# K projections in 64-row TensorE tiles, with the order of a fused linear-attention and gated-FFN kernel drawn anew

## The chip, the cores and the metric

The kernel runs on one core of a Trainium2 chip. The metric is the device time of one execution in microseconds (us), as the median of several executions. Before the change it is 396.28 us (three runs, 396.02 to 397.35). The profiled execution has a span of 394.4 us from its first to its last instruction.

## The reference, cut to what matters

The program is an attention layer without a softmax over the sequence, followed by a gated feed-forward network (FFN). There are 8 batches, 8 heads, 576 rows a head, head dimension 64 and 128 features.

```python
def phi(x):                                  # q and k alike
    proj = np.einsum('bhsd,df->bhsf', x, w_phi)          # 64 -> 128
    proj = proj - np.max(np.abs(proj), axis=-1, keepdims=True)
    return np.concatenate([np.exp(proj), np.exp(-proj)], axis=-1)
q_p, k_p = phi(q), phi(k)
kv  = einsum('bhsf,bhsd->bhfd', k_p, v);  z = sum(k_p, axis=2)
out = (q_p @ kv) / (q_p @ z + 1e-06)
...
gate = np.maximum(x @ w_gate, 0.0);  val = x @ w_val     # 512 -> 1536, on 4608 rows
return gate * val @ w_out                                # 1536 -> 512
```

The contraction of the projection (`x @ w_phi`) is only 64 deep, while TensorE has 128 rows. That mismatch is what the change is about.

## The kernel before

The work is cut into small pieces: K projections, scaled V, K-by-V products, Q projections, numerators, half-steps of the FFN. A class `Plan` holds for each piece a list of engines with rough durations and the buffers that it takes and frees. The order in which the pieces are issued is a literal list of numbers, `ORDER`, which was annealed offline on that model and is replayed when the kernel is built. All PSUM tiles come from one pool of eight banks.

A K item is four transposed blocks of K. A block has 128 partitions: the 64 dimensions of one chunk of rows in partitions 0 to 63 and those of another chunk in 64 to 127. `w2` is a block-diagonal matrix: `w_phi` in the upper left half, `w_phi` in the lower right half, zeros elsewhere. So one full 128-row matmul of 256 columns projects both chunks, and half of what it multiplies is zero. A K item is issued in two pieces of two matmuls and one bank each:

```python
def project_rows(T2, m):                     # K, before: 128-row matmuls with zeros
    pp = psum_a()
    for i in range(2):
        nc.tensor.matmul(pp[:, 2*F*i : 2*F*(i+1)],
                         lhsT=T2[:, i, :], rhs=w2.rearrange("p a f -> p (a f)"))   # L287
    nc.vector.tensor_reduce(m, pp..., op=ALU.max, apply_absolute_value=True)       # L292
    return pp

def k_rows(st, i):                           # called for i = 0 and i = 1
    pp = project_rows(st["T"][:, 2*i : 2*i+2], st["m"][:, 4*i : 4*i+4])
    kp = st["pool"].tile([P, 2, 4, F], BF16, name=f"kp{i}")
    for s, sign in ((0, 1.0), (1, -1.0)):
        nc.scalar.activation(kp[:, s]..., pp, AF.Exp, scale=sign)                  # L322
    ...
    if i == 1:                               # the row factors, once for the item
        ek = ...; two small nc.scalar.activation(ek[:, :, s], st["m"], AF.Exp)     # L329
```

Q already uses 64-row tiles. A Q group first projects by columns (two matmuls of 512 columns, one for each half of the rows), then by rows (eight matmuls of 128 columns, alternating between the upper and the lower 64 rows, each half into its own bank):

```python
def q_group(st, i, places, first):
    ...
    for par in range(2):
        rows = slice(D*par, D*(par+1))
        nc.tensor.matmul(cols[par]..., lhsT=w2[rows, par, :], rhs=T4[rows])        # L382
    banks = [psum_a(), psum_a()]
    for j in range(4):
        for par in range(2):
            rows = slice(D*par, D*(par+1))
            nc.tensor.matmul(banks[par][:, F*j : F*(j+1)],
                             lhsT=T4[rows, j, :], rhs=w2[rows, par, :])            # L389
    ...                                      # 4 exps on ScalarE (L397), 2 row maxima on VectorE
```

The other TensorE lines are the K-by-V products (L363, 20 matmuls an item), the numerators (L420), the first FFN products with the value and the gate weights (L487), the second FFN product (L506), transposes (L267, L459) and filler matmuls on zeros that keep the clock up while nothing else can run in the first 45 us (L840).

In the model, a piece on TensorE had only its own duration:

```python
for i, op in enumerate(ops):
    eng, us = op[:2]
    src = op[2] if len(op) > 2 else i - 1
    t = max(free[eng], ready if src is None or not i else ends[src])
    ...
# K: [("PE", 0.23), ("DVE", 0.6), ("ACT", 0.48, 0), ("ACT", 0.48, 0)], one bank, twice an item
# Q: [("PE", 0.66)] + ..., four banks
```

Of the kernel before, what the change touches and what calls it, by code (L numbers as in the profile page):

```python
# [19 lines left out]
class Plan:  # L20
# [10 lines left out]
    def __init__(self, slots):  # L31
        self.slots = {tag: [0.0] * n for tag, n in slots.items()}
        self.free = dict.fromkeys(self.LAG, 0.0)
        self.done = {}
        self.uses = {}
        self.pieces = []
# [6 lines left out]
    def times(self, piece):  # L43
# [12 lines left out]
        for i, op in enumerate(ops):  # L56
            eng, us = op[:2]
            src = op[2] if len(op) > 2 else i - 1
            t = max(free[eng], ready if src is None or not i else ends[src])
            if len(op) > 4:  # L60
                t = max(t, self.done[op[4]])
            if eng == "NONE":
                t = ready if src is None or not i else ends[src]
            if start is None:
                start = t
            free[eng] = t + us
            ends.append(t + us + (op[3] if len(op) > 3 else self.LAG[eng]))
        return start, ready, ends, free

    def emit(self, piece, got):  # L70
        _, _, fn, ops, _, gives, take, drop, _, at = piece
        _, _, ends, self.free = got
        for tag in take:
            self.slots[tag].pop(0)
# [14 lines left out]
    def order(self):  # L89
# [3 lines left out]
        for i in map(int, ORDER.split()):  # L93
            piece = self.pieces[i]
            got = self.times(piece)
            assert got is not None
            now, start = self.free["PE"], got[0]
            if piece[3][0][0] == "PE" and start < self.BUSY_TILL and self.slots["pa"][0] <= now:
                n = int((start - now - 0.25) / (0.43 if now < 8.0 else 0.22))
                if n > 0:  # L100
                    self.slots["pa"].append(self.slots["pa"].pop(0))
                    got = self.times(piece)
                    yield lambda n=n: self.keep_busy(n)
            yield self.emit(piece, got)


ORDER = """40 41 42 0 1 4 45 55 46 50 56 43 57 58 47 51 2 60 61 7 48 62 52 63 65 76 53 66 3 59 64 10 49 87 92
67 54 102 44 93 5 88 94 72 6 8 73 74 95 89 68 69 97 70 77 78 96 71 75 107 90 83 14 79 439 80 13 91
440 9 81 84 85 441 442 443 444 445 446 447 448 103 143 449 82 11 141 86 450 12 98 99 451 118 452
149 453 454 455 100 456 457 458 104 459 17 460 108 461 159 101 462 463 105 129 464 465 109 466 106  # L110
467 136 468 110 111 112 469 470 471 114 472 115 473 474 116 119 475 154 120 476 477 137 478 121 150
125 479 15 480 18 16 138 113 126 130 481 122 123 127 155 142 186 164 482 483 131 484 485 124 23 144
486 117 128 156 151 160 188 139 132 21 487 488 489 145 490 491 492 152 493 157 161 494 146 495 147
133 19 496 497 153 165 162 158 498 134 193 499 166 20 198 140 22 148 500 163 189 194 501 171 199
167 502 503 195 168 200 504 169 505 506 507 230 175 508 244 187 509 190 510 170 172 196 173 174 203
176 191 231 511 201 219 512 242 177 204 205 197 513 182 178 206 208 514 515 183 179 516 245 180 184
181 202 185 28 192 232 207 517 24 237 238 239 518 27 250 233 25 519 209 246 520 521 234 522 210 523
235 255 260 524 26 525 32 211 526 212 527 215 528 135 529 247 287 213 251 530 531 532 236 248 533
256 534 535 304 261 536 241 537 240 538 262 214 539 540 220 216 541 542 543 221 263 544 545 243 217
276 546 252 249 289 226 218 253 227 264 547 33 228 229 257 222 265 258 548 549 223 224 305 550 551  # L120
299 225 552 266 254 553 554 306 555 294 267 259 300 556 557 29 307 558 31 295 301 559 268 272 560
345 288 561 562 343 346 563 269 270 564 565 566 302 567 296 273 34 568 277 271 569 570 571 309 572
297 278 573 290 274 574 575 283 35 576 279 284 577 578 285 308 579 580 356 581 280 582 275 281 310
298 291 583 584 286 585 311 586 351 303 292 282 587 588 347 293 357 589 590 30 316 338 591 312 592
339 344 593 340 313 361 594 320 348 36 314 595 596 597 331 598 599 600 321 38 388 601 341 602 603
604 605 358 366 606 359 607 317 322 608 332 318 609 610 352 323 611 612 353 613 324 614 615 333 390
315 354 616 617 327 618 325 362 328 319 360 326 329 619 620 363 330 621 355 334 39 622 349 623 624
367 391 625 626 350 627 432 628 389 364 368 335 405 365 629 630 336 395 369 410 631 370 371 632 433
633 406 377 634 37 635 407 636 637 373 342 638 639 396 640 641 642 643 374 378 644 400 645 372 397
398 337 646 647 379 648 649 392 375 650 384 399 401 393 651 385 652 653 654 386 394 380 421 402 381  # L130
655 656 657 382 387 411 376 658 408 383 659 660 412 661 662 409 663 403 664 404 665 666 413 417 667
668 669 414 415 670 671 672 673 674 422 675 676 677 423 678 418 679 680 681 682 428 683 424 429 684
430 685 686 419 687 688 416 420 689 690 434 431 425 426 691 692 693 435 427 694 695 696 697 698 699
700 701 702 436 703 704 705 706 707 708 709 710 711 712 713 714 715 716 717 718 719 720 721 722 723
724 725 726 437 438 727 728 729 730 731 732 733 734 735 736 737 738 739 740 741 742 743 744 745 746
747 748 749 750 751 752 753 754 755 756 757 758 759 760 761 762 763 764 765 766 767 768 769 770 771
772 773 774"""
# [6 lines left out]
def kernel(  # L144
# [138 lines left out]
    def project_rows(T2, m):  # L283

        pp = psum_a()
        for i in range(2):
            nc.tensor.matmul(  # L287
                pp[:, 2 * F * i : 2 * F * (i + 1)],
                lhsT=T2[:, i, :],
                rhs=w2.rearrange("p a f -> p (a f)"),  # L290
            )
        nc.vector.tensor_reduce(  # L292
            m,
            pp.rearrange("p (c f) -> p c f", f=F),
            axis=AX.X,
            op=ALU.max,
            apply_absolute_value=True,
        )
        return pp

# [11 lines left out]
    def k_start(st, T, pool):  # L312
        st["T"] = T
        st["pool"] = pool
        st["kp"] = []
        st["m"] = sb_s.tile([P, 8], FP32, name="mk")

    def k_rows(st, i):
        pp = project_rows(st["T"][:, 2 * i : 2 * i + 2], st["m"][:, 4 * i : 4 * i + 4])
        kp = st["pool"].tile([P, 2, 4, F], BF16, name=f"kp{i}")  # L320
        for s, sign in ((0, 1.0), (1, -1.0)):
            nc.scalar.activation(  # L322
                kp[:, s].rearrange("p c f -> p (c f)"), pp, AF.Exp, scale=sign
            )
        st["kp"].append(kp)
        if i == 1:
            ek = st["ek"] = sb_s.tile([P, 8, 2], FP32, name="ek")
            for s, sign in ((0, -1.0), (1, 1.0)):
                nc.scalar.activation(ek[:, :, s], st["m"], AF.Exp, scale=sign)  # L329
# [19 lines left out]
    def k_kv(st, b, u, copy):  # L349
# [4 lines left out]
        for hh in range(2):  # L354
            h = 2 * u + hh
            for s in range(2):
                for c in range(C + 1):
                    if c < C:
                        lhsT, rhs = st["kp"][hh][:, s, c, :], st["vs"][:, 4 * hh + c, s, :]
                    else:  # L360
                        lhsT = mixed["kp"][h // 4][:, s, h % 4, :]
# [13 lines left out]
    def q_group(st, i, places, first):  # L375
# [9 lines left out]
        banks = [psum_a(), psum_a()]  # L385
        for j in range(4):
            for par in range(2):
                rows = slice(D * par, D * (par + 1))
                nc.tensor.matmul(  # L389
                    banks[par][:, F * j : F * (j + 1)], lhsT=T4[rows, j, :], rhs=w2[rows, par, :]  # L390
                )
# [189 lines left out]
    def k_pieces(rank, st, start, ops, needs, take, name, late=()):  # L581
        plan.add(rank, "kT", start, ops, needs, (rank, "T"), take, late)
        for i in range(2):
            ops = [("PE", 0.23), ("DVE", 0.6), ("ACT", 0.48, 0), ("ACT", 0.48, 0)]
            if i == 1:
                ops.append(("ACT", 0.4, 1))
            plan.add(
                rank,
                "krows",
                lambda i=i: k_rows(st, i),  # L590
                ops,
                [(rank, "T")],
                (rank, "rows", i),
                ["pa"],
                [("pa", 3)] + [(tag, 0, n, key) for tag, n, key in name],
                [(rank, "rows", 0)] if i else [],
            )

    def k_item(rank, b, u):
# [14 lines left out]
        if by_dma:  # L614
            k_pieces(
                rank, st, start, [("NONE", 0.0)], [("knT", b)], ["kp"], [(f"knT{b % 2}", 2 * NU, b)]
            )
        else:
# [7 lines left out]
                [("T4", 2, rank)],  # L626
# [7 lines left out]
            [(rank, "rows", 1), (rank, "rows", 0), ("vn", b, u == 0) if b == 0 else ("vn", b)],  # L634
# [15 lines left out]
    def k_item_mixed(rank, i):  # L650
# [11 lines left out]
        if by_dma:  # L662
            k_pieces(rank, st, start, [("NONE", 0.0)], [("kmT", i)], ["km"], [("kmT", 2, i)])
        else:
# [7 lines left out]
                [("T4", 2, rank)],  # L672
                [("pa", 1), ("kmn", 0)],
            )
        for bb in range(2):
# [6 lines left out]
                [(rank, "rows", 1), (rank, "rows", 0), ("vm", i)],  # L682
# [4 lines left out]
    def q_pieces(rank, turned, ops, needs, take, late, name, cols, chunks, first, by_dma):  # L687
# [7 lines left out]
        for i, places in enumerate(cols):  # L695
# [7 lines left out]
                [("PE", 0.66)]  # L703
# [266 lines left out]
```

## Time and profile before

| what | value |
|---|---|
| time, median of 3 | 396.28 us |
| span of the profiled execution | 394.4 us, 8456 instructions |
| TensorE clock granted, mean | 0.998 |
| VectorE busy | 254.1 us |
| ScalarE busy | 245.3 us |
| GpSimd busy | 156.3 us |
| DMA | 45.04 MB, 114 GB/s on average |

The page lists busy times of each engine (PE is TensorE, PEld its weight loads, DVE VectorE, ACT ScalarE, POOL GpSimd), the span in 40 slices, the chain of work that ended last, and groups of instructions by source line, with what ended the idle time before them. A matmul's duration in such a list includes its way through the array, which overlaps with its successor; what a block of matmuls costs TensorE is therefore read from the start of the block to the start of the next one, which the timeline gives.

### The profile page before, as it was taken

How to read it: one execution, taken by the hardware profiler on the slowest of the kernel's cores; microseconds unless marked ns; L12 is line 12 of the kernel's file. 1: busy time of each engine (PE TensorE's matmuls, PEld its weight loads, DVE VectorE, ACT ScalarE, POOL GpSimd, SP SyncE). 2: the span in 40 equal slices, each digit the busy share in tenths (PEclk: the TensorE clock that was granted, in tenths of full speed). 3: DMA queues.
4: the chain of work that ended last, by engine and by line, in shares of the span. 5: the costliest groups of instructions: out<-in, count | busy, mean ns of one | idle time of the engine just before them, and what ended most of it. 6: DMA issues, size and time to landing. Idle time of an engine off the chain costs nothing.

```text
span 394.4 us, 8456 instructions
## 1 busy us (share of the span) xinstructions
PE 378.1 (96%) x3220; PEld 207.1 (53%) x3269; DVE 254.1 (64%) x570; ACT 245.3 (62%) x563; POOL 156.3 (40%) x202
## 2 busy tenths in 40 slices
PE   6978999999999999999999999999999999999994
PEld 3566855556556545544555455555554444444442
DVE  2789767868988969667746776777736744422420
ACT  2887584688988677777486766578647333323321
POOL 2899652268574365625252437225511210010000
PEclk9999999999999999999999999999999999999999
DMA  7989999999958992599559705630220031011003
GB/s 227 196 147 193 178 154 132 182 167 215 121 102 157 302 162 55 109 172 228 82 93 193 89 15 95 173 82 2 56 95 13 6 89 55 0 53 69 0 22 84
DMA packets 91801, 45.04 MB, mean 114 GB/s; under 512 B 57842, under 2 KB 87154, under 8 KB 91762
## 3 DMA queue, kind: packets, MB, share of 16 engines
q1 hardware_dynamic: 62994, 30.88, 36.7%
q0 software_dynamic: 28768, 13.63, 29.3%
q8 instruction: 25, 0.41, 0.4%
q14 instruction: 14, 0.11, 0.1%
HBM read 37.81 MB, written 9.44 MB: 120 GB/s over the span
## 4 chain that ended last, share of the span: by engine, by line
PE 88%; POOL 5%; DVE 2%; issue 2%; ACT 1%; DMA 1%; SPq 0%; ACTq 0%; DVEq 0%
PE pf L487 46%; PE pf L506 24%; PE pa L420 5%; PE pa L363 4%; PE pa L287 3%; PE pa L382 3%; PE pa L389 2%; POOL vs L304 2%; DMA wf<-in_w_phi_dram 1%; ACT kp L322 1%; POOL vsm L304 1%; DVE mk L292 1%; DVE h L498 1%; POOL wv_sb L251 1%; PE pa L267 1%
## 5 line engine op out<-in xcount | busy, mean ns | idle before, releaser
L498 DVE SCALAR_TENSOR_TENSOR h<-pf,val_sb 128x512 bf16<-128x512 f32 (+1 forms) x114 | 74.5, 658 | 67.4 <-PE pf L487 46.7
L496 ACT CAST val_sb<-pf 128x512 bf16<-128x512 f32 (+1 forms) x114 | 63.9, 576 | 62.7 <-PE pf L487 59.3
L322 ACT ACTIVATE kp<-pa 128x512 bf16<-128x512 f32 x144 | 77.5, 607 | 39.1 <-DVE mk L292 38.9
L506 PE MATMUL pf<-wo_sb,h 128*128 128x512 bf16 x412 | 98.8, 379 | 1.0
L487 PE MATMUL pf<-xT,wg_sb 128*128 128x512 bf16 (+1 forms) x397 | 98.9, 366 | 0.7
L487 PE MATMUL pf<-xT,wv_sb 128*128 128x512 bf16 (+1 forms) x392 | 98.3, 366 | 0.7
L449 POOL TENSOR_TENSOR xu<-u,r 128x512 bf16<-128x512 f32 x36 | 37.4, 1042 | 146.0 <-DVE r L447 65.3
L304 POOL TENSOR_TENSOR vs<-vn,ek 128x512 bf16<-128x512 f32 x64 | 65.8, 1050 | 27.7 <-ACT ek L329 27.7
L397 ACT ACTIVATE qp<-pa 128x512 bf16<-128x512 f32 x128 | 66.4, 623 | 4.5 <-PE pa L382 4.5
L487 PEld LDWEIGHTS <-wv_sb 128*128 128x128 bf16 x456 | 42.5, 98 | 42.2 <-DMA out_dram<-out_sb 0.2
L487 PEld LDWEIGHTS <-wg_sb 128*128 128x128 bf16 x456 | 42.2, 98 | 40.1 <-issue 0.3
L506 PEld LDWEIGHTS <-h 128*128 128x128 bf16 x432 | 40.0, 98 | 41.4
L292 DVE TENSOR_REDUCE mk<-pa 128x4 f32<-128x512 f32 x72 | 47.7, 679 | 10.5 <-PE pa L287 10.2
L275 DVE TENSOR_REDUCE mq<-pa 128x4 f32<-128x512 f32 x72 | 45.7, 680 | 11.6 <-PE pa L389 11.4
L436 DVE TENSOR_TENSOR t<-pa,cq 128x195 f32<-128x195 f32 (+3 forms) x120 | 39.5, 329 | 17.7 <-PE pa L420 17.0
L444 DVE TENSOR_TENSOR u<-pa,t 128x195 f32<-128x195 f32 (+3 forms) x120 | 40.5, 338 | 6.8 <-DVE t L436 0.5
L516 ACT COPY out_sb<-pf 128x512 f32<-128x512 f32 x36 | 21.4, 594 | 32.5 <-PE pf L506 30.3
L420 PEld LDWEIGHTS <-qp 128*128 128x128 bf16 x640 | 30.7, 98 | 14.5 <-issue 0.4
L420 PE MATMUL pa<-kv,qp 128*128 128x65 bf16 x640 | 33.9, 193 | 0.2
L363 PEld LDWEIGHTS <-kp 128*128 128x128 bf16 x640 | 22.3, 98 | 4.7 <-ACT kp L322 1.1
L363 PE MATMUL pa<-vs,kp 128*128 128x65 bf16 x512 | 23.7, 193 | 0.8 <-ACT kp L322 0.8
L304 POOL TENSOR_TENSOR vsm<-vm,ekm 128x512 bf16<-128x512 f32 x16 | 16.4, 1049 | 12.9 <-DVE ekm L339 6.9
(64 smaller groups left out, 264.2 us busy)
## 6 DMA issues: line engine op xcount, KB each, us to landing
out_dram<-out_sb SPq DMA_DIRECT2D x32, 256.0 KB, 2.6
vn<-in_v_dram SPq DMA_DIRECT2D x7, 1024.0 KB, 8.7
qn<-in_q_dram POOLq DMA_DIRECT2D x8, 512.0 KB, 8.0
kn<-in_k_dram POOLq DMA_DIRECT2D x7, 512.0 KB, 7.0
wv_sb<-in_moe_w_val_dram POOLq DMA_DIRECT2D x3, 512.0 KB, 8.0
wg_sb<-in_moe_w_gate_dram POOLq DMA_DIRECT2D x3, 512.0 KB, 9.0
wo_sb<-in_moe_w_out_dram POOLq DMA_DIRECT2D x1, 1536.0 KB, 18.4
vm<-in_v_dram SPq DMA_DIRECT2D x8, 128.0 KB, 5.1
```

Of the source, the lines that this page charges most:

```text
L275: nc.vector.tensor_reduce(m, bank.rearrange("p (c f) -> p c f", f=F), axis=AX.X, op=ALU.max, apply_absolute_value=True,)
L292: nc.vector.tensor_reduce(m, pp.rearrange("p (c f) -> p c f", f=F), axis=AX.X, op=ALU.max, apply_absolute_value=True,)
L304: eng.tensor_tensor(dst[:, :, s, 0:D], src, ek[:, :, s : s + 1].to_broadcast([P, 8, D]), op=ALU.mult,)
L322: nc.scalar.activation(kp[:, s].rearrange("p c f -> p (c f)"), pp, AF.Exp, scale=sign)
L363: nc.tensor.matmul(kv_ps[:, hh, s, :], lhsT=lhsT, rhs=rhs, start=(n == 0), stop=(n == 19))
L397: nc.scalar.activation(x["qp"][:, s, slot].rearrange("p a b -> p (a b)"), cols[par], AF.Exp, scale=sign,)
L420: nc.tensor.matmul(pn[:, E * (2 * i + s) : E * (2 * i + s + 1)], lhsT=x["qp"][:, s, slot, blk, :], rhs=kvs[b, h // 2][:, h % 2, s, :],)
L444: nc.vector.tensor_tensor(x["u"][rows, lo : lo + n], ab[:, :, 0], t, op=ALU.add)
L487: nc.tensor.matmul(ps, lhsT=w[:, dc, P * fi : P * fi + P], rhs=xT[:, dc, lo:hi], start=(dc == 0), stop=(dc == NDC - 1),)
L496: nc.scalar.copy(st["val"], ps)
L498: nc.vector.scalar_tensor_tensor(st["h2"][:, fi, lo:hi], ps, 0.0, st["val"], op0=ALU.max, op1=ALU.mult)
L506: nc.tensor.matmul(st["po"], lhsT=st["h2"][:, fi, P * t : P * t + P], rhs=wo_sb[:, fi, :], start=(fi == 0), stop=(fi == NFC - 1),)
```

## The change

K is projected like the row part of Q: four blocks and both halves in one piece of eight 64-row matmuls on two banks. The purpose is to multiply no zeros: the two halves of the array work on the two chunks at the same time. `project_rows` goes, `q_group` shares the new helper, and the two `kp` tiles of an item become one.

```diff
-    def project_rows(T2, m):
-        ...
+    def rows_group(T4):
+        banks = [psum_a(), psum_a()]
+        for j in range(4):
+            for par in range(2):
+                rows = slice(D * par, D * (par + 1))
+                nc.tensor.matmul(
+                    banks[par][:, F * j : F * (j + 1)], lhsT=T4[rows, j, :], rhs=w2[rows, par, :]
+                )
+        return banks
+
+    def k_group(st):
+        banks = rows_group(st["T"])
+        kp = st["kp"] = st["pool"].tile([P, 2, 4, 2, F], BF16, name="kp")
+        for par in range(2):
+            row_max(st["m"][:, par::2], banks[par])
+            for s, sign in ((0, 1.0), (1, -1.0)):
+                nc.scalar.activation(
+                    kp[:, s, :, par, :],
+                    banks[par].rearrange("p (a f) -> p a f", f=F),
+                    AF.Exp, scale=sign,
+                )
+        ek = st["ek"] = ...                       # as before, after both halves
...
-        lhsT, rhs = st["kp"][hh][:, s, c, :], st["vs"][:, 4 * hh + c, s, :]
+        lhsT = st["kp"][:, s, 2 * hh + c // 2, c % 2, :]
```

The model behind the order learns of a switch between 128-row and 64-row tiles, and K and Q pieces are marked as of the second kind:

```diff
+            if eng in ("PE", "PE64"):
+                us += 0.1 * (eng != self.mode)
+                eng = "PE"
...
-        for i in range(2):
-            ops = [("PE", 0.23), ("DVE", 0.6), ("ACT", 0.48, 0), ("ACT", 0.48, 0)]
...
+            [("PE64", 0.23)]
+            + [("DVE", 0.6, 0), ("ACT", 0.48, 0), ("ACT", 0.48, 0)] * 2
+            + [("ACT", 0.4, 4)],
...
-                [("PE", 0.66)]
+                [("PE64", 0.45)]
```

`ORDER` is annealed anew: 739 pieces in place of 775, since each of the 36 K items is one piece now. Nothing else of the computation, the loads or the buffers changes. In the built program, TensorE's order differs as follows: 576 row matmuls of 64 rows in place of 288, no more K matmuls of 128 rows and 256 columns (144 before), 43 fillers in place of 41, all other counts equal. Stretches of consecutive 64-row matmuls: 35 before, 59 after.

## Prediction

> **What bounds the kernel now.** I read the engine shares first, then the chain that ended last, then the busy time by stretch, and last the timeline of TensorE where K and Q pieces stand.
>
> ```profile
> PE 378.1 (96%) x3220; PEld 207.1 (53%) x3269; DVE 254.1 (64%) x570; ACT 245.3 (62%) x563; POOL 156.3 (40%) x202
> PE   6978999999999999999999999999999999999994
> PE 88%; POOL 5%; DVE 2%; issue 2%; ACT 1%; DMA 1%; SPq 0%; ACTq 0%; DVEq 0%
> ```
>
> TensorE is busy in nine tenths or more of almost every slice and holds 88% of the chain. Only the first four slices (some 40 us) are different.
>
> ```profile
> 37.30:60.00 22.70, 21.72 (x252) 16.35 (x251) 16.03 (x40) 14.95 (x39) 13.04 (x18) 1.00 1.39 171
> 60.00:100.00 40.00, 39.68 (x390) 22.72 (x395) 33.03 (x79) 29.51 (x71) 20.64 (x26) 1.00 1.13 167
> 100.00:300.00 200.00, 198.28 (x1789) 107.69 (x1819) 144.18 (x325) 143.20 (x333) 90.11 (x112) 1.00 0.67 118
> 300.00:389.00 89.00, 88.47 (x481) 41.51 (x490) 34.57 (x70) 30.50 (x56) 4.17 (x4) 1.00 0.12 37
> ```
>
> The columns are the stretch, its length, and the busy time of PE, PEld, DVE, ACT and POOL. From the first FFN product (37.3) on, the uncovered TensorE time is 0.98 + 0.32 + 1.72 + 0.53 = 3.6 us. So after 37.3 a microsecond of TensorE work saved is a microsecond of the kernel saved, and better ordering alone can win at most 3.6 us there.
>
> The price of each block, from its start to the next start:
>
> ```profile
> 144.89 0.38 PE L287 MATMUL pa<-w,knT 128*128 128x256 bf16 x2
> 145.11 1.03 PE L487 MATMUL pf<-xT,wv_sb 128*128 128x512 bf16 x4
> 145.97 1.03 PE L487 MATMUL pf<-xT,wg_sb 128*128 128x512 bf16 x4
> 146.93 0.39 PE L382 MATMUL pa<-qnT,w 64*128 64x512 bf16 x2
> 147.16 0.39 PE L389 MATMUL pa<-w,qnT 64*128 64x128 bf16 x8
> 147.47 0.36 PE L420 MATMUL pa<-kv,qp 128*128 128x65 bf16 x6
> ```
>
> Half a K item costs 145.11 - 144.89 = 0.22 us, so an item 0.44. An FFN half-step costs 0.86 (0.215 a matmul of 512 columns), but 0.96 when a 64-row block follows it: entering 64-row tiles costs 0.10. Two concurrent 512-column matmuls cost 0.23. The row block of Q costs 0.31 to 0.32. Its four pairs stream 4 x 128 = 512 columns, which at 0.215 leaves 0.10 for going back to 128-row tiles. I went through all such blocks after 60 us: entry is 0.09 to 0.10 after FFN, K-by-V and numerators alike, and the row block is 0.31 to 0.32 in nearly all 30 cases. TensorE's weight loads show the same switch as idle time, 0.4 us for each Q group:
>
> ```profile
> PEld L382 <- issue: 10.3, 25, 0.4
> ```
>
> **What the Trainium skill says.** "TensorEngine Tiling (Array Packing)", Key Properties, says that different tiles can load weights and multiply in parallel, and that changing the tiling mode (not just the tile) drains TensorE. The trace agrees with both: two 512-column matmuls in 0.23 us, and 0.10 us at each border. Its Gotcha 1: PSUM Pressure says that different row tiles write to different banks. This is why a K piece now takes two banks at once. Its PSUM Bottleneck says that tiling speeds up TensorE but not the emptying of PSUM; the four exps and two row maxima of an item are indeed as many as before. "TensorE: Matmul & The Clock Gate", in the part on 56 ns against 53.3 ns, gives 215.7 ns from start to start for 512 columns; the trace has 0.86 / 4 = 0.215.
>
> **The change part by part.**
>
> 1. K's matmuls. Of 36 items, 7 are projected before the first FFN product and 29 after it, in both orders. The 29 cost 29 x 0.44 = 12.8 us now. As 64-row pairs they stream 29 x 0.22 = 6.4 us. That is -6.4 us.
>
> 2. Switches. A K item alone between 128-row blocks costs 0.10 + 0.22 + 0.10 = 0.42 in place of 0.44: almost nothing is won. It pays only where it touches a Q group or another K item, and saves 0.20 there. I counted the stretches of 64-row matmuls in the two built orders. Before: 35, of them 3 ahead of the first FFN product. After: 59, of them 10 ahead of it. So the part bound by TensorE has 49 stretches in place of 32, and pays 17 x 0.20 = +3.4 us. Parts 1 and 2 together: -3.0 us, less than half of the streaming gain. The new order merges only 12 of the 61 groups there (29 K and 32 Q).
>
> 3. Work moved across the start. Before the first FFN product the new order does eight transposes fewer; they cost 8 x 0.055 = +0.4 us later (a block of eight takes 36.47 - 36.02 = 0.45). K-by-V products (100) and numerators (44) ahead of it are as many as before.
>
> 4. The start. Here GpSimd and the chain of dependences set the pace, not TensorE:
>
> ```profile
> 13.34 2.06 ACT kp L322 x4
> 15.40 0.10 ACT ek L329
> 15.57 1.27 POOL vs L304 x2
> ...
> 31.14 1.08 POOL xu L449
> ...
> 35.40 0.62 PE pa L459 x8
> 36.02 0.45 PE pa L267 x8
> 36.47 0.65 PE pa L840 x3
> 37.11 0.38 PE pa L420 x12
> 37.49 0.44 PE pf L487 x4
> ```
>
> Before, the second item's factors come only after the first exps of the third item, and GpSimd idles until 15.57; with an item in one piece the four exps and the factors stand together, so it could start about 1 us earlier. I let most of that be lost again, because up to the first `xu` GpSimd's new order also issues the second mixed K load (1.4 us, from the timeline at 37.4) in place of one weight load (0.75). After the second `xu` (ends 35.35), the old order puts eight transposes and three fillers (0.45 + 0.65 us) ahead of the first FFN product; the new one has 20 K-by-V matmuls between the two transposes of `xu`, and one filler. The first FFN product could come up to 1 us earlier. I book -0.5 us.
>
> 5. ScalarE and VectorE. Same number of exps (144), row maxima (72) and factors (72), and the same sizes. The exps write runs of 128 with gaps; that costs nothing I can see in the profile, so 0. What changes is that they come in one burst: about 2.1 us of exps (13.34: four in 2.06) and 0.4 of factors at once, where two halves were apart.
>
> Sum: -3.0 + 0.4 - 0.5 = -3.1 us. For bursts I add back 0.3: 396.3 - 2.8 = 393.5 us.
>
> **The rivals.** *Bursts take the gain.* A K item next to a Q group asks for up to six of eight banks and puts eight exps (about 4.1 us) in front of the value copies that FFN needs. Then TensorE would wait where it hardly waits now. For it: before, value copies and gates stand close behind TensorE. Against it: ScalarE is busy 143 of 200 us in the middle, and the merged stretches are mostly put before second FFN products, which hold one bank for 2.6 us and need no copy until their end. If it holds, idle time after 37.3 grows from 3.6 to perhaps 6 us, and the time is about 396. *Nothing at the borders.* If row pairs of K did not run at the same time, or a switch cost more than 0.10, the 49 stretches would eat everything: 0.16 us a switch in place of 0.10 adds 2 us for Q and K alike. The Q blocks speak against it: the same helper, the same shapes, the same 0.32. *The order wins more.* The new annealing may also close the early gap (0.98 us before 60) and start FFN a full microsecond earlier: about 392.
>
> **Range and chances.** The TensorE count is safe to about half a microsecond; the start is open by 1 us either way, and new idle time by 1.5 us, mostly upwards. That gives 393.5, with 391.6 to 395.7 for eight times in ten. Two per cent would be 388.4 or 404.2. The first needs all idle time after 37.3 gone besides; the second needs a lost buffer or a stall of several microseconds. So: faster 0.02, within 2% 0.96, slower 0.02.
>
> **What would show it.** K row blocks alone should cost 0.32 from start to next start, and 0.22 when another 64-row block follows; the block before a stretch should be 0.10 longer. The first FFN product should start between 36 and 37.5. From there to the last matmul it should be about 349.5 us in place of 352. PE busy should fall by some 3 us or less. I am wrong if the row blocks of K take about 0.44 (no concurrency), if waits for ScalarE show up before FFN matmuls with more than 2 us in sum, or if FFN starts after 38.

## The result and the profile after

The changed kernel takes 392.51 us (median of four runs, 391.98 to 393.08) against 396.15 for the kernel before in the same series. The ratio is 0.9904, with a 95% interval of 0.9878 to 0.9929: 3.6 us less, within 2%. The prediction was 393.5, with 391.6 to 395.7.

Engine shares and the chain of the changed kernel, from its page:

```profile
PE 377.9 (97%) x3415; PEld 201.3 (52%) x3415; DVE 251.6 (64%) x570; ACT 244.9 (63%) x563; POOL 156.1 (40%) x202
PE 83%; DVE 6%; DMA 3%; ACT 3%; issue 2%; POOL 1%; SPq 0%; DVEq 0%; POOLq 0%; ACTq 0%
```

TensorE still bounds it. The page before lists 3220 matmuls beside 3269 weight loads; here both are 3415. So 49 matmul records were missing before, and busy times of TensorE can't be compared between the two pages. The busy time by stretch (columns as in the prediction) shows the same:

```profile
35.50:60.00 24.50, 24.24 (x296) 17.97 (x296) 19.66 (x50) 16.98 (x45) 13.67 (x18) 1.00 1.43 189
60.00:100.00 40.00, 40.00 (x413) 21.90 (x412) 31.79 (x74) 29.89 (x69) 22.94 (x30) 1.00 0.84 155
100.00:300.00 200.00, 199.03 (x1905) 104.41 (x1904) 143.21 (x324) 145.00 (x337) 87.01 (x108) 1.00 0.68 118
300.00:385.30 85.30, 85.30 (x467) 39.83 (x464) 31.95 (x65) 26.05 (x46) 4.17 (x4) 1.00 0.13 40
```

The uncovered time is 1.2 us here. Part of the 3.6 us that I read as gaps before was only missing records.

A ledger that does not depend on busy times: I priced every TensorE block by its start-to-start time (a full-width FFN matmul 0.2156 us, a half-width one or an old K matmul 0.109, a K-by-V product 0.0303, a numerator 0.0318, a transpose 0.055, a column matmul of Q 0.115, a 64-row row matmul 0.0275, each border of a 64-row stretch 0.10), counted the blocks in the built order, and call the rest of the measured time waits. As a rest, the waits also hold any error of the prices, so tenths of a microsecond there say little. Each row of such a table comes from one profiled execution. All from the first FFN product to the start of the last 48 matmuls:

| | first FFN product starts | from there to the last block | priced work | waits |
|---|---|---|---|---|
| before | 37.33 | 341.60 | 339.7 | 1.9 |
| after | 35.53 | 339.80 | 337.3 | 2.5 |

The start gave 1.8 us, the work 2.4, and waits took 0.6; the span fell by 394.4 - 390.7 = 3.7.

The timeline of TensorE in the changed kernel, at a K item that stands alone, and at two K items together:

```profile
98.28 0.54 PE L415 MATMUL pa<-kv,qp 128*128 128x65 bf16 x12
98.75 0.40 PE L309 MATMUL pa<-w,knT 64*128 64x128 bf16 x8
99.08 1.04 PE L482 MATMUL pf<-xT,wg_sb 128*128 128x512 bf16 x4
```

```profile
131.60 1.03 PE L482 MATMUL pf<-xT,wv_sb 128*128 128x512 bf16 x4
132.56 0.62 PE L309 MATMUL pa<-w,knT 64*128 64x128 bf16 x16
133.11 1.04 PE L482 MATMUL pf<-xT,wg_sb 128*128 128x512 bf16 x4
```

A lone item costs 0.33 from start to next start, and the block before it 0.09 to 0.10 extra (12 numerators take 0.47, and 0.38 elsewhere; the four FFN matmuls before 132.56 take 0.96). Two items together cost 0.55: the second adds only 0.22.

GpSimd in the start of the changed kernel, with the first FFN product below:

```profile
13.46 0.81 POOL L255 DMA_DIRECT2D wg_sb<-in_moe_w_gate_dram  x1
14.29 2.06 POOL L290 TENSOR_TENSOR vs<-vn,ek 128x512 bf16<-128x512 f32 x2
29.99 1.06 POOL L444 TENSOR_TENSOR xu<-u,r 128x512 bf16<-128x512 f32 x1
33.15 1.04 POOL L444 TENSOR_TENSOR xu<-u,r 128x512 bf16<-128x512 f32 x1
35.53 0.60 PE L482 MATMUL pf<-xT,wv_sb 128*128 128x256 bf16 x4 [0.27 <-DVE xT L460]
```

and the last two of these before the change:

```profile
34.29 1.05 POOL L449 TENSOR_TENSOR xu<-u,r 128x512 bf16<-128x512 f32 x1
37.33 0.60 PE L487 MATMUL pf<-xT,wv_sb 128*128 128x256 bf16 x4
```

The second scaling of V begins at 14.29 in place of 15.57, and a weight load now fills what was an idle gap. The first `xu` comes 1.15 us earlier (31.14 before). From the second `xu` to the first FFN product it is 35.53 - 33.15 = 2.38 us in place of 37.33 - 34.29 = 3.04.

### The profile page after: what moved, and what is told of

It is laid out like the page before. It is cut to its first block, busy times and chain, and to the rows that moved or that the text cites. A ratio compares the mean times of both kernels' runs of the same rounds, so it can differ in the third digit from the quotient of the medians.

```text
span 390.7 us, 8804 instructions
## 1 busy us (share of the span) xinstructions
PE 377.9 (97%) x3415; PEld 201.3 (52%) x3415; DVE 251.6 (64%) x570; ACT 244.9 (63%) x563; POOL 156.1 (40%) x202
## 4 chain that ended last, share of the span: by engine, by line
PE 83%; DVE 6%; DMA 3%; ACT 3%; issue 2%; POOL 1%; SPq 0%; DVEq 0%; POOLq 0%; ACTq 0%
PE pf L482 46%; PE pf L501 20%; PE pa L364 4%; PE pa L415 4%; PE pa L309 4%; PE pa L383 2%; ACT kp L321 2%; DMA out_dram<-out_sb 2%; DVE mq L279 1%; DVE u L439 1%; DMA wf<-in_w_phi_dram 1%; DVE mk L279 1%; DVE t L431 1%; PE pa L271 1%; PE pa L832 1%
## 5 line engine op out<-in xcount | busy, mean ns | idle before, releaser
L501 PE MATMUL pf<-wo_sb,h 128*128 128x512 bf16 x432 | 101.0, 379 | 0.0
L482 PE MATMUL pf<-xT,wv_sb 128*128 128x512 bf16 (+1 forms) x408 | 99.6, 366 | 0.9 <-DMA out_dram<-out_sb 0.6
L444 POOL TENSOR_TENSOR xu<-u,r 128x512 bf16<-128x512 f32 x36 | 37.5, 1044 | 152.9 <-DVE r L442 108.6
L321 ACT ACTIVATE kp<-pa 128x512 bf16<-128x512 f32 x144 | 74.6, 615 | 21.0 <-DVE mk L279 20.6
L501 PEld LDWEIGHTS <-h 128*128 128x128 bf16 x432 | 38.9, 98 | 42.1
L279 DVE TENSOR_REDUCE mk<-pa 128x4 f32<-128x512 f32 x72 | 45.5, 682 | 7.0 <-PE pa L309 7.0
L511 ACT COPY out_sb<-pf 128x512 f32<-128x512 f32 x36 | 21.5, 602 | 37.5 <-PE pf L501 36.0
L415 PEld LDWEIGHTS <-qp 128*128 128x128 bf16 x640 | 29.9, 98 | 15.7 <-issue 0.7
L364 PE MATMUL pa<-vsm,kp 128*128 128x65 bf16 x128 | 20.6, 193 | 0.4 <-POOL vsm L296 0.4
```

What stands on the lines that cost most here:

```text
L279: nc.vector.tensor_reduce(m, bank.rearrange("p (c f) -> p c f", f=F), axis=AX.X, op=ALU.max, apply_absolute_value=True,)
L321: nc.scalar.activation(kp[:, s, :, par, :], banks[par].rearrange("p (a f) -> p a f", f=F), AF.Exp, scale=sign,)
L364: nc.tensor.matmul(kv_ps[:, hh, s, :], lhsT=lhsT, rhs=rhs, start=(n == 0), stop=(n == 19))
L415: nc.tensor.matmul(pn[:, E * (2 * i + s) : E * (2 * i + s + 1)], lhsT=x["qp"][:, s, slot, blk, :], rhs=kvs[b, h // 2][:, h % 2, s, :],)
L482: nc.tensor.matmul(ps, lhsT=w[:, dc, P * fi : P * fi + P], rhs=xT[:, dc, lo:hi], start=(dc == 0), stop=(dc == NDC - 1),)
L501: nc.tensor.matmul(st["po"], lhsT=st["h2"][:, fi, P * t : P * t + P], rhs=wo_sb[:, fi, :], start=(fi == 0), stop=(fi == NFC - 1),)
```

## The experiments

The theory: the tiles are worth their streaming time less 0.20 us for each stretch, about 3 us in the new order; the rest comes from an earlier start. The main rivals: the fresh order does it all; or the tiles do it in any order.

**e1: the new order without the tiles.** K goes back to four 128-row matmuls on the same two banks, in the same piece and order. The maxima and exps keep their number and sizes and take the columns as these matmuls lay them out.

```diff
-        banks = rows_group(st["T"])
+        banks = [psum_a(), psum_a()]
+        for j in range(4):
+            nc.tensor.matmul(banks[j // 2][:, 2*F*(j % 2) : 2*F*(j % 2 + 1)],
+                             lhsT=T4[:, j, :], rhs=w2.rearrange("p a f -> p (a f)"))
```

> The changed kernel and its order to the letter, but K is projected by four 128-row matmuls of 256 columns with the zeros in them, as before the change, on the same two banks in the same piece. Theory (the tiles are worth their streaming time less the switches): after the first FFN product 29 K items cost 0.44 in place of 0.22 us (+6.4), and 17 stretches of 64-row tiles go (49 to 32, -3.4), so +3.0: about 395.5 us, with the first FFN product at 35.5 us as in the changed kernel. Rival (the new order alone won the time, the tiles are a wash): 392.5 us.

Measured: 395.29 us, ratio to the kernel before 0.9968 (0.9956 to 0.9979). First FFN product at 35.83, then 342.28 to the last block (priced 340.1, waits 2.1). So the tiles are worth 2.8 us in this order by the medians (2.5 by the ratios and by the stretch after the first FFN product, 342.28 less 339.80), and the early start does not need them. The rival "the order alone" gets some 1 us of the 3.6.

**e2: the two halves one after the other.**

```diff
-        for j in range(4):
-            for par in range(2):
+        for par in range(2):            # for K alone; Q as before
+            for j in range(4):
```

> The changed kernel, but K's eight matmuls go first through the four blocks of the upper 64 rows and then through the four of the lower, in place of alternating. Theory (the gain in streaming is two halves at work at the same time, and matmuls are taken in order): only the fourth and fifth overlap, an item's row block costs some 0.17 to 0.22 us more, times 29 items: +4.8 to +6.4 us, 397.3 to 398.9 us, and alone between 128-row blocks it is dearer than the old 0.44. Rival (a 64-row matmul is quicker by itself, whatever its neighbour): no change, 392.5 us.

Measured: 392.62 us, ratio 0.9906 (0.9869 to 0.9943), as the changed kernel. What I expected of my own theory failed. The timeline of e2:

```profile
98.09 0.41 PE L311 MATMUL pa<-w,knT 64*128 64x128 bf16 x8
98.44 1.04 PE L484 MATMUL pf<-xT,wg_sb 128*128 128x512 bf16 x4
```

The block costs 0.35, hardly more than 0.33. In narrow windows around the block at 96.41, the eight starts lie at about 96.41, .42, .47, .49, .53, .54, .58 and .60, in pairs although four matmuls of one half stand first in the program, and in the compiled instructions of TensorE too. The trace's semaphores fit: only the first matmul of each half waits for a bank, and these two start first and second; only the last of each half signals, and these two start seventh and eighth. Either the halves overlap whatever the order, or they do not overlap at all and the matmuls are simply short. This run can't tell; e9 was made for that.

**e9: both halves' work on one half.**

```diff
-                rows = slice(D * par, D * (par + 1))
-                ... banks[par] ..., lhsT=T4[rows, j, :], rhs=w2[rows, par, :]
+                rows = slice(0, D)      # for K alone
+                ... banks[par] ..., lhsT=T4[rows, j, :], rhs=w2[rows, 0, :]
```

It leaves the lower chunks of K out and projects the upper ones twice; shapes, counts and places stay.

> The changed kernel, but all eight matmuls of a K item use the upper 64 rows: the chunks in the lower half are left out and those of the upper half are projected twice, into the same two banks (the output is not the reference's). Every instruction has the shape and place of the changed kernel. Theory (the gain is the two halves of the array at work at the same time, in whatever order they are given): the block loses it, its start-to-start goes from 0.32 to 0.53 or so, 29 items at 0.22 us: +6.4 us, about 398.9 us. Rival (a 64-row matmul of 128 columns is just short, and nothing runs side by side): 392.5 us.

Measured: 399.52 us, ratio 1.0062 (1.0041 to 1.0082). The timeline of e9:

```profile
144.17 1.02 PE L483 MATMUL pf<-xT,wv_sb 128*128 128x512 bf16 x4
145.13 0.62 PE L310 MATMUL pa<-w,knT 64*128 64x128 bf16 x8
145.68 1.04 PE L483 MATMUL pf<-xT,wg_sb 128*128 128x512 bf16 x3
```

(The last row counts three matmuls in 1.04 us: a fourth record is missing.) The same eight matmuls now cost 0.55 in place of 0.33, from 145.13 to 145.68, and two items together 1.0 in place of 0.55. The gain is the two halves side by side. Together with e2: a matmul of the other half starts beside the first one even when it stands four places further on.

**e3: the weight load out of the gap.** In the order, one number moves by one place, behind the second scaling of V:

```diff
-... 42 49 6 46 7 54 ...
+... 42 49 46 6 7 54 ...
```

> The changed kernel, but the one weight load that GpSimd now issues in its idle gap at 13.5 us is issued after the second scaling of V instead; nothing else moves. Theory (GpSimd's queue sets the start of the FFN, and a microsecond there is one of the kernel): the gap stays empty, and 0.8 us of issue moves into the full stretch: first xu at 30.8 in place of 30.0, first FFN product at 36.3 in place of 35.5, time +0.8: about 393.3 us. Rival (the start hangs on something else, such as ScalarE's exps or the loads): the first FFN product stays at 35.5 and the time at 392.5 us.

Measured: 393.21 us, ratio 0.9904 (0.9874 to 0.9934). The medians differ by 0.7 us in the expected direction, but the intervals of the two ratios are nearly the same, so the time does not decide. The trace says more. GpSimd of e3,

```profile
14.12 2.06 POOL L290 TENSOR_TENSOR vs<-vn,ek 128x512 bf16<-128x512 f32 x2 [0.67 <-ACT ek L329]
30.79 1.06 POOL L444 TENSOR_TENSOR xu<-u,r 128x512 bf16<-128x512 f32 x1
```

has its gap of 0.67 back, the first `xu` comes at 30.79 (29.99 before the edit), the first FFN product at 36.34 (35.53), and the stretch from there to the last block is 339.80 in both. These are single executions, in which GpSimd's first copy also comes at different times. Counted from that copy, the FFN begins after 28.59 us in e3, and after 27.30 to 28.02 in the six others with the changed kernel's start (the kernel itself, e1, e2, e9, e10 and e11), so the loss stands clear of this scatter. GpSimd's queue sets the start, and what it loses there is still missing at the last block.

**e4: the tiles in the old order.** The changed kernel with the order of before; each K item stands in one piece where its second half stood.

```diff
-ORDER = """0 40 41 1 44 45 4 52 ...
+ORDER = """40 41 0 1 4 44 52 48 42 ...        # the old order, renumbered
```

> The changed kernel with the order of the kernel before: each K item stands in one piece where its second half stood, all else as in the old order. Theory (most of the win needs the new order): after the first FFN product there are 59 stretches of 64-row tiles in place of the old 32, so -6.4 + 27 x 0.20 = -1.0 us against the kernel before, and the start keeps the eight transposes and the fillers ahead of the FFN; with a stall or two from two banks at once: 395 to 396.5 us. Rival (the tiles bring the win in any order): 392.5 us.

Measured: 401.16 us, ratio 1.0113 (1.0086 to 1.014): 5 us slower than before, worse than either side expected. First FFN product at 39.79, then 344.98 (priced 338.8, waits 6.1). TensorE in e4, at a Q group behind a K item:

```profile
113.24 0.39 PE L383 MATMUL pa<-qnT,w 64*128 64x512 bf16 x2
113.47 0.22 PE L309 MATMUL pa<-w,qnT 64*128 64x128 bf16 x1
114.37 0.38 PE L309 MATMUL pa<-w,qnT 64*128 64x128 bf16 x7 [0.69 <-ACT kp L321]
```

The first row matmul of Q has a bank; the second must wait 0.69 us for a bank that K's exps still hold. These are the waits of the "bursts" rival: after the first FFN product the trace puts 2.8 us of TensorE's idle time down to K's exps, against 0.8 before the change and none in the changed kernel.

**e5: the piece without the tiles, in the old order.** The body of e1 with the order of e4.

> The kernel of e4_tiles_alone (a K item in one piece where its second half stood in the old order), but with the old 128-row matmuls of 256 columns. It asks what made that kernel slower than the one before. Theory A (the piece: two banks, and four exps in a row where the order had been annealed for halves): the waits stay, only the 0.9 us between tiles and their switches is paid back the other way: about 402 us, with the FFN again starting near 39.8 us. Theory B (the many switches of the tile mode made it slow): without them about 396 to 397 us.

Measured: 401.25 us, ratio 1.0112 (1.0085 to 1.0139), equal to e4. First FFN product at 38.31, 1.5 us earlier than I had expected, then 345.56 (priced 339.7, waits 5.9, of which the trace puts 2.2 us down to K's exps). Theory A holds in the main: what costs 5 us is the item in one piece, on two banks and at that place, where the order had been made for halves. The tiles in 59 stretches win next to nothing there: the later part is 0.6 us shorter with them, where the prices say 0.9 (338.8 against 339.7), and the equal time includes a later start.

**e6 and e7: other new orders.** Only `ORDER` differs from the changed kernel.

```diff
-ORDER = """0 40 41 1 44 45 4 52 ...
+ORDER = """...                          # annealed anew; two draws
```

> The changed kernel with another order, annealed by myself on the same kind of model, with a price for switches. By counting its instructions: after the first FFN product 43 stretches of 64-row tiles in place of 49 (-1.2 us), two K items fewer there (9 ahead of the FFN in place of 7: -0.4) and eight transposes fewer (-0.4). Theory (each switch is 0.20 us of the time): 2.0 us less from the first FFN product to the end, so about 390.5 us if start and waits are alike. Rival (merged stretches make bursts that TensorE then waits for): the waits grow by what the switches save, 392.5 us or more.

> As e6_new_order with a second order from another draw: 45 stretches after the first FFN product (-0.8 us against the changed kernel), 9 K items, eight transposes and six numerators ahead of the FFN that stood after it (-0.4, -0.4, -0.2): 1.8 us less from there to the end, so about 390.7 us if start and waits are alike; 392.5 us or more if waits take it back.

Measured: e6 395.16 us (ratio 0.9964, 0.9949 to 0.9979), e7 395.75 (0.9966, 0.9946 to 0.9987). Both miss my number by 5 us. In e6 the priced work fell by 2.1 us as counted (335.2), but waits rose to 5.0 and the FFN began at 37.67. In e7 the later part is the best of all runs with 336.70 us (priced 335.4, waits 1.3), 3.1 less than the changed kernel; but its FFN begins at 40.31. The later part of e7 fits the price of a border, and shows that merging need not make waits; the start was lost.

**e8: the kernel before with an order annealed in the same way.**

> The kernel before, 128-row K matmuls in two halves and all, with an order annealed anew in the same way and for as long as those of e6 and e7. It is the control for what a fresh order is worth without the tiles. By counting: still 32 stretches of 64-row tiles after the first FFN product, but two K items (-0.9), 20 K-by-V products (-0.6) and four numerators (-0.1) moved ahead of it: 1.6 us less from there to the end. Theory (fresh order is worth a microsecond or two to either kernel, and the tiles come on top): 394 to 395.5 us, some 3 to 4 us over e6 and e7. Rival (the order is all that counts): within 1 us of e6 and e7.

Measured: 397.60 us, ratio 1.0027 (1.0016 to 1.0038), with the FFN from 38.56 on and 341.78 to the last block (priced 338.1, waits 3.7). This is slower than the order of before, where I had expected 394 to 395.5: my orders are not as good as the author's, for either kernel. Among mine, the tiles kernel is ahead by 1.9 to 2.4 us in the medians (e6 and e7 against e8), less than the 3 to 4 expected, and in the later part by 1.6 to 5.1. Two draws stand here against one, and two draws alone differ by 3.5 in the later part (e6 and e7), so e8 agrees with e1 but measures the tiles less well.

**e12: more fillers in e7.** In e7, TensorE stood idle from about 32.1 to 33.8, and then ran at half clock.

```diff
                 n = int((start - now - 0.25) / (0.43 if now < 8.0 else 0.22))
+                if n > 0 and now > 29.0:
+                    n += 7
```

> e7_new_order2 with seven more filler matmuls (1.5 us at full clock) in the one gap at 31.7 to 33.8 us in which TensorE waited there for GpSimd; after that gap the granted clock had read 0.51 from 35 to 40 us. Nothing else differs. Theory (the late start of e4, e5 and e7 is in good part TensorE at half clock after it had idled): the clock stays near 1.0, the blocks from 34 to 40 us take some 2 us less, the first FFN product comes near 38.3 us in place of 40.3, and the time falls by about 2 us to 393.5 or so. Rival (GpSimd and the exps set that start, the clock is a bystander): the first FFN product stays at 40 us or comes later by the fillers, and the time stays near 395.7 us.

Busy time by stretch of e7, and below of e12 (the granted clock is the third figure from the end of a row, TensorE's busy time the second figure of time, behind the stretch's length):

```profile
30.00:35.00 5.00, 2.52 (x35) 1.53 (x33) 4.57 (x16) 3.89 (x13) 4.88 (x7) 0.81 1.30 193
35.00:40.00 5.00, 4.68 (x71) 3.71 (x68) 4.05 (x7) 5.00 (x12) 5.00 (x7) 0.51 1.26 207
```

```profile
30.00:35.00 5.00, 3.89 (x48) 2.28 (x47) 4.76 (x17) 4.69 (x13) 4.26 (x6) 1.00 1.36 202
35.00:40.00 5.00, 3.88 (x85) 3.36 (x83) 4.70 (x12) 5.00 (x15) 5.00 (x8) 1.00 1.43 199
```

The clock stays at 1.00, and the first FFN product comes at 38.44 in place of 40.31, as expected. But most of these 1.87 us are not the clock's: the first `xu` of GpSimd already comes at 31.57 in place of 32.64, on account of work that ended before the added fillers ran (its first copy alone is at 8.19 in place of 8.84). From that `xu` to the first FFN product it is 6.87 us in place of 7.67, so the clock is worth 0.8 us at most. Also, the second K-by-V item behind the first FFN product waits 1.2 us for GpSimd at 39.6, so waits rise to 2.7. Time 394.01 us, ratio 0.9956 (0.9935 to 0.9977). The median is 1.7 us below e7, but the two intervals overlap: the trace shows that the fillers keep the clock up, and what this is worth in time is not settled.

**e10 and e11: the author's start, the rest annealed.** The first 85 or 120 pieces of the changed kernel's order are kept.

> The changed kernel and the first 85 pieces of its order (until some microseconds after the first FFN product), the rest annealed anew. By counting: 45 stretches of 64-row tiles after the first FFN product in place of 49 (-0.8 us), all other counts as in the changed kernel. Theory (e7_new_order2 lost its better later part to a late start, and the start comes back with the old beginning): the first FFN product at 35 to 36 us, waits down from 2.5 towards 1.3 us as in e7: about 390.5 us. Rival (the start and the rest can't be had together): 392.5 us or more.

> As e10_kept_start, with the first 120 pieces kept and another draw: 46 stretches after the first FFN product (-0.6 us). About 390.7 us by the theory, 392.5 us or more by the rival.

Measured: e10 392.31 us (ratio 0.9887, 0.9867 to 0.9908), e11 392.83 (0.99, 0.9881 to 0.9918). The start came back (35.80 and 35.92), but the time is that of the changed kernel within the intervals: the rival holds. The profiled run of e10 was its slowest (395.43; the other four took 392.2 to 392.5), and shows where that execution lost time, in ScalarE and the DMA queue of SyncE:

```profile
170.71 0.59 ACT L511 COPY out_sb<-pf 128x512 f32<-128x512 f32 x1 [4.87 <-DMA out_dram<-out_sb]
171.34 0.44 PE L415 MATMUL pa<-kv,qp 128*128 128x65 bf16 x6 [2.46 <-ACT out_sb L511]
```

Two output writes took 5.79 us to be issued (from 165.86 on); the next copy needed one of the two output buffers that they read and waited 4.87 us, and TensorE 2.46 us for the bank that the copy empties. A third buffer was not tried. No run here beats the changed kernel beyond its interval.

All runs in one table (us; medians, and from the profiled run the rest):

| kernel | time | FFN starts | to the last block | priced | waits |
|---|---|---|---|---|---|
| e1 order alone | 395.29 | 35.83 | 342.28 | 340.1 | 2.1 |
| e2 halves apart | 392.62 | 34.81 | 339.55 | 337.3 | 2.3 |
| e3 load late | 393.21 | 36.34 | 339.80 | 337.3 | 2.5 |
| e4 tiles alone | 401.16 | 39.79 | 344.98 | 338.8 | 6.1 |
| e5 piece alone | 401.25 | 38.31 | 345.56 | 339.7 | 5.9 |
| e6 new order | 395.16 | 37.67 | 340.18 | 335.2 | 5.0 |
| e7 new order 2 | 395.75 | 40.31 | 336.70 | 335.4 | 1.3 |
| e8 before, new order | 397.60 | 38.56 | 341.78 | 338.1 | 3.7 |
| e10 kept start | 392.31 | 35.80 | 342.41 | 336.5 | 5.9 |
| e11 kept start 2 | 392.83 | 35.92 | 339.54 | 336.7 | 2.9 |
| e12 fillers | 394.01 | 38.44 | 338.15 | 335.4 | 2.7 |

e9 has 35.31 and 345.13; at the price of the changed kernel (337.3) it has 7.8 us over.

## Why the prediction was right

- *TensorE bounds it after the first FFN product.* Right, and e3 shows it from the other side: a start 0.81 us later left the stretch after it as long as it was. The size of the gaps was wrong. I read 3.6 us; by the ledger 1.9 were waits, and part of the rest was missing matmul records.
- *K's matmuls, -6.4 us.* Right: 0.22 us for an item that follows another 64-row block. e9 takes away the two halves at once, and 6.3 us come back by the ratios (1.0062 less 0.9904, times 396), 7.0 by the medians and 5.3 in the later part of its profiled execution, which was its fastest.
- *Switches, +3.4 us.* Right: 0.09 to 0.10 at each border, before and after. Together with the first term I had -3.0; e1 has 2.8 in the medians and 2.5 in the trace. That a lone K item wins next to nothing shows in e4 against e5: with 59 stretches in place of 32, the tiles shorten the later part by 0.6 us.
- *Eight transposes, +0.4 us.* In the ledger as counted, not tested by itself.
- *The start, -0.5 us.* This term was mis-sized: it measured -1.8. Of this, 0.66 us came after the second `xu` (2.38 in place of 3.04), inside the "up to 1 us" that I had named; 0.9 came on GpSimd between its first copy and the first `xu` (22.1 us in place of 23.0); and 0.25 because the first copy was earlier. The step that failed is "I let most of that be lost again". I weighed a K load of 1.4 us against a weight load of 0.75, and did not see that another weight load moves into the idle gap ahead of the second scaling, so that GpSimd's full stretch grew no longer. e3 puts that load behind the second scaling and loses 0.8 us: then 23.0 us lie between the first copy and the first `xu`, as before the change, so with the gap left empty the step would have held. The 0.25 us (first copy at 7.88 in place of 8.13, when the first K load is there) no change of the order explains: that copy lay between 7.51 and 8.84 in the runs here. The first FFN product stood at 35.53, outside the 36 to 37.5 that I had named.
- *ScalarE and VectorE, 0.* Right: an exp of K takes 615 ns on average with the gaps, and 617 in e1, which writes without them.
- *Bursts, +0.3 us.* Not shown. The ledger's waits rose by 0.6, but after the first FFN product no wait of TensorE in the changed kernel is put down to K's exps; the longest, 0.6 us, is for an output write. The rival of the bursts is real, but the new order avoids it: e4 and e5 have some 4 us more waits than the kernel before, in an order that was not made for two banks at once.
- *The sum.* -2.4 of work with its borders and transposes, -1.8 of start, +0.6 of waits: -3.6, where I had -2.6, -0.5 and +0.3, in sum -2.8. The start was 1.3 us better than booked, and 0.5 of work and waits went the other way; that the total came as near as 0.8 is in part luck. The rival "the order wins more", with the FFN a full microsecond earlier and about 392 us, came nearest to what happened.

So the parts of the change can be weighed: the tiles are worth 2.5 to 2.8 us in the new order and next to nothing in the old; the new order with its one-piece items is worth some 1 us without the tiles; and the change would have lost time if the order had not been drawn anew, since one K item in one piece, where I put it, costs 5 us in the old one. What stays open is how much of this last is the late start (2.5 us in e4, 1.0 in e5, both partly at a clock of 0.54 and 0.64 from 35 to 40 us) and how much the place I chose for the piece; other places were not tried.

## What to carry to other kernels

Halving the streaming time with row tiles pays only where a stretch of such tiles is long enough: here a border pair costs 0.20 us and an item saves 0.22, so count the stretches in the built order before counting the matmuls. When a scheduled kernel's piece changes its shape (one bank to two, half a burst to a whole one), the old order is part of what was tuned, and must be drawn anew before the change is judged. And look at the start apart from the rest: there, an empty slot in the queue that paced it was worth about its full length.

## What the runs showed that I had not expected

- Two row tiles overlap even when the program gives all matmuls of one first (e2: 0.35 us a block against 0.33; e9, with one half only: 0.55). The Trainium skill, "TensorE: Matmul & The Clock Gate", Step-by-step: what each phase is for, says that matmuls stay in program order and only weight loads are pulled ahead. For matmuls on the two halves this case shows otherwise, or at least starts in pairs 0.01 us apart that the program order does not give.
- A gap of under 2 us on TensorE went with half clock (e7: idle from 32.1 to 33.8, and the clock reads 0.50 from 33.1 to 39.9; 1.00 with seven fillers in the gap, e12). In the 3.4 us up to 33.1, TensorE was busy 1.65 us. In e4 and e5 the clock reads 0.54 and 0.64 from 35 to 40 us.
- Issuing on SyncE's queue can take long: 9.04 us for one transposing load in the changed kernel, at 167 us, and 5.79 us for two output writes in e10. TensorE waited for the latter by way of ScalarE's copy.
